# The last wait of a decode block: SyncE's queue or GpSimd's

## The chip, the cores and the metric

The kernel runs on one core of a Trainium2 chip. The metric is the device time of one execution in microseconds. Every comparison is of this time; the profile of one execution says where it goes. Engines carry the profile's names: PE is TensorE, DVE is VectorE, ACT is ScalarE, POOL is GpSimd and SP is SyncE. A q behind a name (SPq, POOLq) means the engine's own queue: waits, semaphores, branches and the issuing of DMAs.

## The reference

One step of decoding for 8 sequences: layer norm, attention over the last 1,024 cached positions (32 query heads, 4 key and value heads of 128), the output projection with a residual, then layer norm and a gated feed-forward block (GELU) with a second residual. All is float32.

```
W = min(4096, max(256, Sk // 4))
q = (x @ wq).reshape(B, Sq, Hq, Dh).transpose(0, 2, 1, 3)
k = repeat(k_cache[:, :, Sk - W:, :], rep, axis=1)
v = repeat(v_cache[:, :, Sk - W:, :], rep, axis=1)
p = softmax(einsum("bhqd,bhkd->bhqk", q, k) * (Dh ** -0.5))
attn = einsum("bhqk,bhkd->bhqd", p, v).transpose(...).reshape(B, Sq, Hq * Dh) @ wo
h = x + attn                                  # x was normalized ahead of wq
h2 = h + (gelu(n @ w_gate) * (n @ w_up)) @ w_down      # n = layernorm(h); Dm 1024, Df 3584
```

## The kernel before

The work is fourteen passes over 111 MB of weights and cache (`q0` to `d1` in `PASSES`), which SyncE's queue loads in turn into the two halves of one SBUF buffer, `w`. A pass's load waits until TensorE has used up the half that it goes into; TensorE multiplies the pass that has landed by a small stationary tile, `st`, into PSUM banks; VectorE, ScalarE and GpSimd turn the sums into the next stationary tile. Each engine has its own instruction stream, written out by hand, and semaphores alone order them: `pe`, `dve`, `act` and `pool` count what their engine has done, `s_in` and `s_dn` count what DMAs have landed.

The end is what the change touches. The last four of the down projection's 28 chunks arrive in small transfers (`s_dn`), and TensorE multiplies each as it lands. VectorE adds the last products to `pre` in two parts of `o_fin`, 160 and 96 columns. Then:

- ScalarE issues the store of the first part (L480) and, when the second is written (`s_fin`), adds 1 to `s_end` (L481).
- SyncE issues the store of the second part when `s_fin` says so (L482, L483).
- GpSimd, when `pre` is done, adds 1 to `s_end` (L485).
- SyncE waits for both counts in `s_end` (L486), clears the program's semaphores up to `s_fin` for the next execution (L487), and waits on L488 until both stores have landed: each adds 16 to `s_out`, and the wait takes the 32 away again.

L488 is the last line of `decode_block`. Lines at 569 are the opening that the framework puts ahead of a program.

Of the kernel before, what the change touches and what calls it, by code (L numbers as in the profile page):

```python
# [115 lines left out]
def decode_block(nc, out, x, srcs, W):  # L116
# [19 lines left out]
    s_out = nc.alloc_semaphore("s_out")  # L136
# [348 lines left out]
    nc.gpsimd.wait_ge(*t_pre).then_inc(s_end, 1)  # L485
    nc.sync.wait_ge(s_end, 2).then_inc(s_end, -2)  # L486
    nc.sync.sem_clear(range(first.num, s_fin.num + 1))  # L487
    nc.sync.wait_ge(s_out, 32).then_inc(s_out, -32)  # L488


# [93 lines left out]
```

## Time and profile before

| | us |
|---|---|
| time before, median of 3 runs | 263.91 |
| lowest and highest of the 3 | 263.84, 263.96 |
| time of the profiled execution | 263.77 |
| its span, from the program's first instruction to its last | 262.46 |
| what of its time lies outside the span | 1.31 |

The span is what all views speak of: they list the program's own instructions. The measured time is longer. The trace also records every change of a semaphore, and these records go on behind the span, where no view lists an instruction. One semaphore, number 2, is not the program's own. After TensorE's work is done it changes 18 times, in two passes of nine:

```
changes of semaphore 2 (ns from the span's start; steps since the change before)
pass 1: 260700  261247  261285  261329  262581  262624  262663  262697  262744
                  +547     +38     +44   +1252     +43     +39     +34     +47
pass 2: 263534  263569  263607  263650  263674  263779  263818  263852  263899
                   +35     +38     +43     +24    +105     +39     +34     +47
last changes of s_out: 262421 (the last of the stores' 32 counts), 262455 (taken away by L488)
```

Between the passes, from 262694 to 263310, nearly all semaphores of the core change once. A pass with the steps of pass 2, within 7 ns each, stands ahead of the program too and ends at 1 ns.

### The profile page before, as it was taken

How to read it: one execution, taken by the hardware profiler on the slowest of the kernel's cores; microseconds unless marked ns; L12 is line 12 of the kernel's file. 1: busy time of each engine (PE TensorE's matmuls, PEld its weight loads, DVE VectorE, ACT ScalarE, POOL GpSimd, SP SyncE). 2: the span in 40 equal slices, each digit the busy share in tenths (PEclk: the TensorE clock that was granted, in tenths of full speed). 3: DMA queues.
4: the chain of work that ended last, by engine and by line, in shares of the span. 5: the costliest groups of instructions: out<-in, count | busy, mean ns of one | idle time of the engine just before them, and what ended most of it. 6: DMA issues, size and time to landing. Idle time of an engine off the chain costs nothing. (4 is left out here: it accounts for less than half of the span.)

```text
span 262.5 us, 2187 instructions
## 1 busy us (share of the span) xinstructions
PE 136.8 (52%) x960; PEld 42.6 (16%) x960; DVE 35.9 (14%) x98; ACT 19.1 (7%) x28; POOL 6.8 (3%) x16
## 2 busy tenths in 40 slices
PE   0005905806826607627708608539277590585954
PEld 0001301201222102122102202112121130121321
DVE  0060110120130210110120100450101004003013
ACT  1030000000020000110000000210401010000000
POOL 2000100000000000000000100000000001001010
PEclk9999975955865965955956965957959598586899
DMA  8998997999899799989979989997999999799996
GB/s 320 484 410 390 479 479 340 459 479 410 390 479 479 340 459 479 420 380 479 479 330 469 479 380 420 479 479 320 479 434 405 439 479 479 320 454 424 439 390 230
DMA packets 3216, 111.31 MB, mean 424 GB/s; under 512 B 496, under 2 KB 784, under 8 KB 1040
## 3 DMA queue, kind: packets, MB, share of 16 engines
q1 hardware_dynamic: 3024, 111.20, 98.4%
q10 hardware_dynamic: 192, 0.11, 0.1%
HBM read 111.18 MB, written 0.13 MB: 424 GB/s over the span
## 5 line engine op out<-in xcount | busy, mean ns | idle before, releaser
L161 PE MATMUL banks<-w,st 128*32 128x512 f32 x864 | 125.3, 743 | 115.7 <-PEq L156 115.7
L161 PEld LDWEIGHTS banks<-w,st 128*32 128x32 f32 x864 | 34.3, 133 | 201.4 <-issue 201.4
L183 PE MATMUL banks<-ident,p 128*128 128x128 f32 x56 | 9.3, 321 | 6.3 <-PEq L156 6.3
L183 PEld LDWEIGHTS banks<-ident,p 128*128 128x128 f32 x56 | 7.4, 164 | 12.3 <-issue 12.3
L358 ACT ACTIVATE p<-banks,nmax 128x1024 f32<-128x1024 f32 x2 | 2.2, 1113 | 73.5 <-DVE nmax L98 73.5
L98 DVE TENSOR_REDUCE nmax<-banks 128x1 f32<-128x1024 f32 x2 | 2.5, 1225 | 33.8 <-PE banks L161 33.8
L98 DVE TENSOR_TENSOR y_sum<-y_sum,banks 128x512 f32<-128x512 f32 (+1 forms) x4 | 2.1, 552 | 33.6 <-PE banks L161 17.8
L98 DVE TENSOR_SCALAR q<-banks 128x512 f32<-128x512 f32 x2 | 1.4, 692 | 31.3 <-PE banks L161 31.3
L98 DVE TENSOR_TENSOR o_sum<-o_sum,banks 128x512 f32<-128x512 f32 x2 | 1.4, 690 | 29.5 <-ACT o_sum L371 29.5
L98 DVE TENSOR_TENSOR d_sum<-d_sum,banks 128x256 f32<-128x256 f32 (+1 forms) x3 | 1.4, 509 | 17.3 <-POOL d_sum L456 12.1
L397 POOL TENSOR_TENSOR y_sum<-y_sum,x_sb 128x256 f32<-128x256 f32 x1 | 0.7, 722 | 115.7 <-ACT y_sum L396 115.7
L422 POOL COPY st<-at 128x768 f32<-128x768 f32 (+2 forms) x3 | 1.8, 609 | 68.4 <-DVE at L98 68.4
L371 ACT COPY o_sum<-banks 128x512 f32<-128x512 f32 x2 | 1.2, 586 | 26.8 <-PE banks L161 26.8
L98 DVE TENSOR_TENSOR u0s<-u0s,banks 128x512 f32<-128x512 f32 x1 | 0.7, 689 | 16.3 <-ACT u0s L412 16.3
L98 DVE TENSOR_TENSOR g0s<-g0s,banks 128x512 f32<-128x512 f32 x1 | 0.7, 689 | 15.8 <-ACT g0s L412 15.8
L292 ACT ACT_TABLE_LOAD x2 | 2.6, 1283 | 1.7 <-POOL ident L264 1.6
L98 DVE TENSOR_TENSOR u1s<-u1s,banks 96x512 f32<-96x512 f32 x1 | 0.7, 683 | 14.0 <-ACT u1s L415 14.0
L221 PE MATMUL banks<-w,at 128*32 128x256 f32 x24 | 1.7, 387 | 1.5 <-DMA w<-weights 1.5
L313 ACT COPY st<-ln_t 128x1024 f32<-128x1024 f32 x2 | 2.1, 1046 | 5.1 <-DVE ln_t L98 5.1
L98 DVE TENSOR_TENSOR g1s<-g1s,banks 96x512 f32<-96x512 f32 x1 | 0.7, 682 | 10.9 <-ACT g1s L415 10.9
L98 DVE SCALAR_TENSOR_TENSOR o<-o_sum,share,o 128x128 f32<-128x128 f32 x6 | 2.1, 352 | 0.2
L412 ACT COPY u0s<-banks 128x512 f32<-128x512 f32 x1 | 0.6, 585 | 18.7 <-PE banks L161 18.7
(64 smaller groups left out, 39.5 us busy)
## 6 DMA issues: line engine op xcount, KB each, us to landing
w<-weights SPq DMA_DIRECT2D x2, 6144.0 KB, 23.5
w<-weights SPq DMA_DIRECT2D x2, 4096.0 KB, 24.5
w<-weights SPq DMA_DIRECT2D x1, 3072.0 KB, 17.0
w<-weights SPq DMA_DIRECT2D x2, 1024.0 KB, 20.1
w<-weights SPq DMA_DIRECT2D x1, 512.0 KB, 21.9
w<-weights SPq DMA_DIRECT2D x1, 320.0 KB, 22.3
w<-weights SPq DMA_DIRECT2D x1, 192.0 KB, 22.3
w<-weights SPq DMA_DIRECT2D x10, 28.9
```

Of the source, the lines that this page charges most:

```text
L98: ins = getattr(self.eng, n.name)(*n.args, **n.kw)
L161: ins = nc.tensor.matmul(bank(2 * s + c // 4)[32 * j:32 * j + 32, :], st[s][:, (c * NQ + j) * 32:(c * NQ + j + 1) * 32], w[:, at:at + N], ...
L183: ins = nc.tensor.transpose(pp[h][:, i], p_sb[:, c * P:(c + 1) * P], ident)
L221: ins = pe(lambda e: e.matmul(bank(7)[32 * j:32 * j + 32, 0:QW], at_[:, q, :], w[:, k:k + QW], start=(q == PAIRED), stop=(q == rows - 2)), ...
L292: t = act(lambda e: e.activation(sd, ve, AF.Sqrt), t_ve)
L313: act(lambda e: e.copy(to[1], wide), t, inc=False).then_inc(s_in[1], 2)
L358: t = act(lambda e: e.activation(p_sb, bank(0, 2), AF.Exp, bias=nmax, accum_out=tot), t)
L371: t = dve(lambda e: e.tensor_add(o_sum, o_sum, bank(3)), act(lambda e: e.copy(o_sum, bank(2)), done(f"v{hb}")))
L397: t = pool(lambda e: e.tensor_add(y_sum[:, 0:QW], y_sum[:, 0:QW], x_sb), t)
L412: t = act(lambda e: e.copy(out[:nb], bank(b)[:nb]), done(name))
L422: return nc.gpsimd.tensor_copy(st[s][:, at:at + n * 64].rearrange("p (c x m) -> p c x m", c=n, x=2), at_[:, c0:c0 + n].unsqueeze(2).to_bro ...
```

## The change

The wait on `s_out`, with the subtraction that goes with it, moves from SyncE's stream to GpSimd's. It stays the last line of the program. Nothing else changes: on every engine the instructions that compute, copy or issue a DMA are the same and stand in the same order. SyncE's last instruction is now the clearing on L487, and GpSimd's is this wait, right behind L485.

```diff
     nc.gpsimd.wait_ge(*t_pre).then_inc(s_end, 1)
     nc.sync.wait_ge(s_end, 2).then_inc(s_end, -2)
     nc.sync.sem_clear(range(first.num, s_fin.num + 1))
-    nc.sync.wait_ge(s_out, 32).then_inc(s_out, -32)
+    nc.gpsimd.wait_ge(s_out, 32).then_inc(s_out, -32)
```

## Rows read from the trace of the kernel before

**Rows 1.** The page: shares of the span by engine, and the weights' DMA queue.
```profile
PE 136.8 (52%) x960; PEld 42.6 (16%) x960; DVE 35.9 (14%) x98; ACT 19.1 (7%) x28; POOL 6.8 (3%) x16
...
q1 hardware_dynamic: 3024, 111.20, 98.4%
...
HBM read 111.18 MB, written 0.13 MB: 424 GB/s over the span
```

**Rows 2.** The chain that ended last, its end: start us, us, what.
```profile
237.35 22.27 DMA w<-weights
259.62 0.04 issue
259.66 0.52 PE banks L229 x8
...
260.28 0.54 DVE o_fin L98 x2
```

**Rows 3.** Busy time by engine in the last 1.5 us, its columns first.
```profile
core 0: us, PE busy (x) PEld busy (x) DVE busy (x) ACT busy (x) POOL busy (x), PEclk, DMA share, GB/s
...
261.00:262.50 1.50, 0.00 (x0) 0.00 (x0) 0.00 (x0) 0.00 (x0) 0.00 (x0) 0.74 0.32 87
```

**Rows 4.** The timeline, the two stores' issues: start us, us, queue and line.
```profile
260.63 0.35 ACTq L480 DMA_DIRECT2D out<-o_fin  x1
260.85 0.35 SPq L483 DMA_DIRECT2D out<-o_fin  x1
```

**Rows 5.** What writes `out`: duration ns min/median/max, first and last start.
```profile
L480 ACTq DMA_DIRECT2D out<-o_fin x1: 348/348/348, 260.6 to 260.6; - x1
L483 SPq DMA_DIRECT2D out<-o_fin x1: 348/348/348, 260.8 to 260.8; - x1
...
DMA to landing us min/median/max: 1.6/1.6/1.6
```

**Rows 6.** Line 488, the wait on the stores; columns as in rows 5.
```profile
L488 SPq EVENT_SEMAPHORE  x1: 17/17/17, 262.4 to 262.4; - x1
```

**Rows 7.** Waits of SyncE's queue, from 259: total us, times, longest.
```profile
SPq L483 <- DVE o_fin L98: 22.6, 1, 22.6
SPq L488 <- SPq L488: 1.1, 1, 1.1
```

**Rows 8.** Line 486, SyncE's wait on `s_end`.
```profile
L486 SPq EVENT_SEMAPHORE  x1: 17/17/17, 261.2 to 261.2; - x1
```

**Rows 9.** Line 487, SyncE's clearing of the semaphores.
```profile
L487 SPq EVENT_SEMAPHORE_RANGE_CLEAR  x1: 58/58/58, 261.3 to 261.3; - x1
```

**Rows 10.** GpSimd's timeline from 249 us to the end: its last work.
```profile
249.73 0.72 POOL L456 TENSOR_TENSOR d_sum<-d_sum,h_sb 128x256 f32<-128x256 f32 x1 [10.38 <-ACT d_sum L455]
256.85 0.39 POOL L390 COPY d_ex<-d_sum 64x256 f32<-64x256 f32 x1 [6.40 <-DVE d_sum L98]
```

**Rows 11.** Line 485, GpSimd's last instruction.
```profile
L485 POOLq EVENT_SEMAPHORE  x1: 17/17/17, 260.0 to 260.0; - x1
```

**Rows 12.** Line 276, two more waits on GpSimd's queue.
```profile
L276 POOLq EVENT_SEMAPHORE  x2: 17/17/17, 2.8 to 2.9; - x2
```

**Rows 13.** Line 481, ScalarE's last instruction.
```profile
L481 ACTq EVENT_SEMAPHORE  x1: 17/17/17, 261.0 to 261.0; - x1
```

**Rows 14.** Line 569, the opening: each engine's drain.
```profile
L569 SPq DRAIN  x1: 7/7/7, 0.0 to 0.0; - x1
L569 DVEq DRAIN  x1: 10/10/10, 0.1 to 0.1; - x1
L569 ACTq DRAIN  x1: 8/8/8, 0.1 to 0.1; - x1
...
L569 POOLq DRAIN  x1: 187/187/187, 0.3 to 0.3; - x1
```

## The prediction, made before the changed kernel ran

> **What bounds the kernel now.** I read the page's shares first. The queue that carries the weights takes 98.4% of the sixteen DMA engines' span, at 424 GB/s, while TensorE is busy 52% of the span and GpSimd 3% [rows 1]. The kernel is therefore bound by its weight stream. Nothing in the change touches that stream, so only the end can answer. I went there next with the chain that ended last: a landing of weights at 259.62 us, the last eight TensorE matmuls, and the two last VectorE sums, which end at 260.82 [rows 2]. The reader is to see that the chain as printed stops there: the remaining 1.64 us of the span hold no arithmetic on any engine. The stretch 261.00 to 262.50 has no busy instruction on any of the five and a DMA share of 0.32, which is the stores [rows 3].
>
> Then the stores. ScalarE issues one at 260.63 and SyncE the other at 260.85; each issue holds its queue for 348 ns and the median time to landing is 1.6 us [rows 4, 5]. The later one lands at 260.85 + 1.6 = 262.45, within rounding the end of the span (262.46). The instruction that sees it is the one that the change moves: the wait on L488, one record of 17 ns at 262.4 [rows 6], for which SyncE's queue stood 1.1 us [rows 7]. So the span ends when the second store has landed, and the wait costs the span 17 ns and nothing more.
>
> Last, what lies behind the span. The profiled execution took 263.77 us against a span of 262.46, so 1.31 us of the measured time lies outside it. No view lists instructions there. The updates of semaphore 2, shown with the time before, do: two passes of nine steps, the first waiting for SyncE (fourth step at 261.329, fifth at 262.581) and the second about a microsecond later. Both come after everything that the program does, and in them the change can cost something.
>
> **The change part by part.**
>
> *Taken from SyncE: one wait of 17 ns* [rows 6]. It is SyncE's last instruction and nothing is queued behind it. What SyncE does before it stays: the store, the wait on `s_end` (17 ns at 261.2) and the clearing of the semaphores (58 ns at 261.3) [rows 8, 9]. SyncE is then through at 261.3 + 0.06 = 261.4, about 1.1 us before the store lands, so its 17 ns leave the path.
>
> *Added to GpSimd: the same wait.* GpSimd's last arithmetic is the copy of 0.39 us at 256.85 [rows 10], and its last instruction is the wait on L485 at 260.0 [rows 11]. So GpSimd stands at the new wait from 260.0 on, long before the landing at 262.45, and is never late for it. Nothing is queued behind it, and nobody in the program waits for GpSimd after L485. A wait on GpSimd takes 17 ns in L485 [rows 11] and in two more on L276 [rows 12], the same as on SyncE. How soon it answers to its semaphore shows in the views to 0.1 us only. Term within the span: 17 − 17 = 0, with ±0.1 us as what the rows can resolve. I take 0, because the cover is complete: whoever looks, the store lands at the same moment.
>
> *Who closes the program.* This is the term that I do not take as nothing. In the first pass of semaphore 2 the five upward steps come at 260.700, 261.247, 261.285, 261.329 and 262.581. The last one follows SyncE's wait (updated at 262.455) by 126 ns; the second follows ScalarE's last instruction, its 17 ns wait on L481 at 261.0 [rows 13]; and four steps come back down 43, 39, 34 and 47 ns apart. So I read the pass as a line with SyncE at its far end, which the engines go up and down one after the other. TensorE starts it, ScalarE is second, and the two steps that follow 38 and 44 ns behind it are those of engines that were already there: VectorE, whose last sum ends at 260.82 [rows 2], and GpSimd, as third and fourth in some order. Before the change the last engine to come stands at the far end, and only the way back is left: 43 + 39 + 34 + 47 = 163 ns. After it the last to come is GpSimd. If GpSimd is third, a step up to the fourth, a step to SyncE and the whole way back remain. Their prices are in the second pass, where nobody is late: 43 + 24 + 105 + 39 + 34 + 47 = 292 ns. Difference: +129 ns. If it is fourth, 24 + 105 + 39 + 34 + 47 = 249 ns, +86 ns. The records don't name the engine of a step, so third is a choice: I take the dearer of two values that differ by 0.04 us. This term is +0.13 us, between +0.09 and +0.13.
>
> The Trainium skill ("Runtime: NRT & Kernel Launch", the section on the preamble and postamble breakdown) describes this as a serpentine over the five engines on the sync-barrier semaphore, about 355 ns, 44 ns a hop times eight. By that flat price two more hops up and down would be an estimate of 0.09 us instead of 0.13. The trace agrees with the sum (263.534 to 263.899 is 365 ns) but not with a flat hop: the turn at the far end took 105 ns where it followed at once, 43 ns where it was awaited.
>
> *GpSimd's own way out.* Between its wait and its step SyncE took 126 ns. GpSimd's is not shown, since it was long there when the line reached it. Below: it takes as long as SyncE, 0; I see no row by which it is quicker. Above: at the opening of the program, line 569, the same kind of instruction is drained in 7 ns on SyncE, 10 ns on VectorE and 187 ns on GpSimd, which had memsets in flight [rows 14]: a difference of 0.18 us if the way out holds such a drain and it costs the same. At the end GpSimd has nothing in flight (its last copy ended 5.2 us before the landing [rows 10]), so I stay near the lower end and take +0.03 us.
>
> *Sum.* Against the profiled execution: 263.77 + 0 (wait) + 0.13 (place in the line) + 0.03 (way out) = 263.93 us. The median of the three runs, 263.91, is 0.14 above the profiled one; the same 0.16 on it gives **264.07 us**, or +0.06%. With the ends of the terms the gain or loss is between 0.09 − 0.10 = −0.01 and 0.13 + 0.18 + 0.10 = +0.41 us, which is 263.90 to 264.32.
>
> **The rivals.** A measurement of this kernel tells a change from none beyond about 0.2%, here 0.53 us; "same" is what stays within it.
>
> *GpSimd's way out is long (slower).* Place: after GpSimd's wait, before its step. For it: GpSimd's drain at the opening was 27 times as long as SyncE's [rows 14], and the way out stood hidden before. Against it: all that is known is that GpSimd, done with its 17 ns at 260.0 [rows 11], had come when the line passed at 261.285 or 261.329, so its way out is at most about 1.3 us; and the two that are shown are short, SyncE's 126 ns and ScalarE's 0.21 us (from 261.0 + 0.02 [rows 13], 261.039 in the records' resolution, to 261.247). At the full 1.27 us instead of 0.126, the time would be 263.91 + 0.13 + 1.14 = 265.18. It decides the sign from 0.53 − 0.13 + 0.126 = 0.53 us of way out on. Chance 0.07.
>
> *SyncE alone ends the measured time (faster).* If what is timed ended with SyncE and did not wait for GpSimd, the end would move from 262.44 to the end of SyncE's clearing at 261.4 [rows 9], a gain of up to 1.06 us: 262.85. For it: 1.1 us is what SyncE stood [rows 7]. Against it: the steps of semaphore 2 show the engines leaving together, and the second pass begins only after the first has come down. Chance 0.03.
>
> *It makes no difference at all.* The passes could lie outside what is timed, or GpSimd's way out could be shorter than SyncE's 126 ns by just what the longer way back costs. Then the landing alone decides, as it did, and the time stays 263.91. For it: the store's 1.6 us [rows 5] are the same whoever waits. Against it: 1.31 us of the measured time lie outside the span, and the first pass is what lies next to it. Chance 0.12.
>
> **How the numbers follow.** The forecast, +0.09 to +0.41 us, has 0.78. Both it and the case of no difference are within 0.2%: 0.90. Slower by over 0.2% is the first rival, 0.07; faster is the second, 0.03. The three runs of before spread over 0.12 us. The range is 263.75 to 264.45: the case of no difference less that spread, 263.91 − 0.12 = 263.79, rounded outward, to the forecast's upper end plus it, 264.32 + 0.12 = 264.44. The two rivals that decide a sign lie outside it, 0.10 together, and I leave another 0.05 for what the views don't show.
>
> **What would show it.** In the changed profile the wait of 17 ns should stand on GpSimd's queue at about 262.4, SyncE's last record should be the clearing at about 261.3, and the span should be 262.5 ± 0.2. Issue, duration and landing of the two stores should be as before. The step of semaphore 2 that was late should be the third or fourth, with two quick ones above it, and the stretch from GpSimd's wait to the first pass's last step should be about 0.45 us (126 + 30 + 292 ns) instead of 0.29 (126 + 163 ns). The forecast is wrong if that stretch exceeds 0.8 us (a long way out), if the closing passes do not move with GpSimd (then SyncE alone counts), or if the stores land later, which would be a cause that I have not named.

## The result and the profile after

The changed kernel takes 264.62 us (median of 10 runs, 264.30 to 264.97) against 263.90 (10 runs): ratio 1.0027, 95% interval 1.0019 to 1.0035, slower by 0.72 us. The profiled execution took 264.58 us with a span of 262.70.

The page's shares and the weights' queue first, against [rows 1]: the weights flow as before. TensorE's busy time differs between the two executions (136.8 and 130.0 us); the weights' queue fills the span in both, and nothing here rests on it.

```profile
PE 130.0 (49%) x960; PEld 40.8 (16%) x960; DVE 35.9 (14%) x98; ACT 19.1 (7%) x28; POOL 6.8 (3%) x16
...
q1 hardware_dynamic: 3024, 111.20, 98.3%
...
HBM read 111.18 MB, written 0.13 MB: 424 GB/s over the span
```

The end of the chain that ended last (start us, us, what), against [rows 2]:

```profile
237.16 22.70 DMA w<-weights
259.86 0.04 issue
259.90 0.52 PE banks L229 x8
...
260.52 0.52 DVE o_fin L98 x2
```

Behind the last landing the same pieces follow, with durations within 0.02 us of those before; they end at 261.04, 0.22 us later. The two stores on the timeline, and what writes `out`, against [rows 4, 5]:

```profile
260.88 0.35 ACTq L480 DMA_DIRECT2D out<-o_fin  x1
261.07 0.35 SPq L483 DMA_DIRECT2D out<-o_fin  x1
```

```profile
L480 ACTq DMA_DIRECT2D out<-o_fin x1: 347/347/347, 260.9 to 260.9; - x1
L483 SPq DMA_DIRECT2D out<-o_fin x1: 347/347/347, 261.1 to 261.1; - x1
...
DMA to landing us min/median/max: 1.6/1.6/1.6
```

Issue (347 ns for 348) and landing are unchanged. The moved wait, line 488, against [rows 6], and SyncE's last instruction, line 487, against [rows 9]:

```profile
L488 POOLq EVENT_SEMAPHORE  x1: 17/17/17, 262.7 to 262.7; - x1
```

```profile
L487 SPq EVENT_SEMAPHORE_RANGE_CLEAR  x1: 58/58/58, 261.5 to 261.5; - x1
```

The wait is still 17 ns, seen when the second store lands (261.07 + 1.6). The reader is to see that the rows of the program's end are as they were, 0.25 us of span aside, and that these rows do not make 0.72 us: 264.58 − 262.70 = 1.88 us now lie outside the span, against 1.31 before. That is 0.56 us (1.876 − 1.315), and it is where no view looks. It is so in every run: in the 10 runs of the changed kernel the time less the span is 1.86 to 1.98 us. The records of semaphore 2 do:

```
pass 1, ns from the span's start      step 1  step 2  step 3  step 4  step 5  and back
before (SyncE waits)                  260700  261247  261285  261329  262581  262624  262663  262697  262744
after (GpSimd waits)                  260929  261487  263271  263315  263338  263428  263468  263502  263548
last instruction ends: before 262455 (SyncE), after 262704 (GpSimd)
```

The late step is the third, with two quick ones above it, so GpSimd is third in the line. But it comes 263271 − 262704 = 567 ns after GpSimd's wait, where SyncE's came 126 ns after its own.

The remaining 0.16 us of the 0.72 lie in the span (0.25 between the two profiled executions). The first matmuls on TensorE's timeline, before:

```profile
22.72 3.62 PE L161 MATMUL banks<-w,st 128*32 128x512 f32 x16 [22.72 <-PEq L156]
```

and after:

```profile
22.97 3.60 PE L161 MATMUL banks<-w,st 128*32 128x512 f32 x17 [22.97 <-PEq L156]
```

The difference of the two spans is complete when the first load has landed, 240 us ahead of the instruction that was changed. The repeats below take it up.

### The profile page after: what moved, and what is told of

Same layout as the page of the kernel before. It is cut to its first block, busy times and chain, and to the rows that moved or that the text cites. A ratio compares the mean times of both kernels' runs of the same rounds, so it can differ in the third digit from the quotient of the medians.

```text
span 262.7 us, 2187 instructions
## 1 busy us (share of the span) xinstructions
PE 130.0 (49%) x960; PEld 40.8 (16%) x960; DVE 35.9 (14%) x98; ACT 19.1 (7%) x28; POOL 6.8 (3%) x16
## 5 line engine op out<-in xcount | busy, mean ns | idle before, releaser
L161 PE MATMUL banks<-w,st 128*32 128x512 f32 x864 | 119.4, 713 | 122.7 <-PEq L156 122.7
L161 PEld LDWEIGHTS banks<-w,st 128*32 128x32 f32 x864 | 33.2, 128 | 203.4 <-issue 203.4
L183 PE MATMUL banks<-ident,p 128*128 128x128 f32 x56 | 8.5, 300 | 6.3 <-PEq L156 6.3
L183 PEld LDWEIGHTS banks<-ident,p 128*128 128x128 f32 x56 | 6.7, 152 | 12.3 <-issue 12.3
L396 ACT COPY y_sum<-banks 128x512 f32<-128x512 f32 x1 | 0.6, 586 | 19.3 <-PE banks L161 19.3
```

The costliest lines, as they stand in the source:

```text
L161: ins = nc.tensor.matmul(bank(2 * s + c // 4)[32 * j:32 * j + 32, :], st[s][:, (c * NQ + j) * 32:(c * NQ + j + 1) * 32], w[:, at:at + N], ...
L183: ins = nc.tensor.transpose(pp[h][:, i], p_sb[:, c * P:(c + 1) * P], ident)
L396: t = act(lambda e: e.copy(y_sum, bank(0)), done("o0"))
```

## The experiments

The edits are to the kernel before. Each replaces or surrounds the last wait. In the table behind them, "way out" is the time from the end of the waiting engine's last instruction to its step, "rest" from there to the last step of pass 1; each is read from one profiled execution.

**ScalarE, VectorE, TensorE wait.** Three runs, each with another engine's name:

```diff
-    nc.sync.wait_ge(s_out, 32).then_inc(s_out, -32)
+    nc.scalar.wait_ge(s_out, 32).then_inc(s_out, -32)      # or nc.vector, nc.tensor
```

> ScalarE waits for the stores. Theory A (the engines leave in a line, and each has its own way out between its last wait and its step): ScalarE is second, so its step is late, four quick steps up and the whole way back follow: 38+43+24+105+39+34+47 = 330 ns against 163 with SyncE, and its way out is the 208 ns seen before against 126. The stretch from the wait to the end of the first pass is about 0.54 us (0.29 with SyncE, 0.84 with GpSimd) and the time about 263.90 + 0.25 = 264.15. Rival B (anybody but SyncE is dear, because SyncE leaves the program early): as with GpSimd, about 264.6. The start of the span, by A, has nothing to do with it: span 262.5 and runs within 0.15 us of each other; if the scatter of the spans over 0.6 us is due to SyncE leaving early, it is here too.

> VectorE waits for the stores. Theory A: VectorE is fourth in the line, 24+105+39+34+47 = 249 ns from its step to the end of the first pass against 163; its way out has not been seen, I expect between SyncE's 126 and ScalarE's 208: stretch 0.38 to 0.46 us, time 264.0 to 264.1. Rival B (anybody but SyncE is dear): about 264.6. Scatter of spans: small by A, about 0.6 us if SyncE leaving early causes it.

> TensorE waits for the stores. Theory A (place in the line, and a way out of each engine's own): TensorE is first, so the whole line of 365 ns is left behind its step, against 163 with SyncE; its way out has not been seen, I expect 0.13 to 0.17 us as on the three others that are short. Stretch from the wait's end to the end of the first pass 0.50 to 0.54 us, against 0.29, so the measured time lies 1.53 to 1.57 us above the span (1.32 with SyncE) and the median is about 264.17. Rival D (the way out is long on every engine that stands at the far side of the line from SyncE): 264.5 or more.

Line 488 of each, ScalarE:

```profile
L488 ACTq EVENT_SEMAPHORE  x1: 17/17/17, 262.6 to 262.6; - x1
```

VectorE:

```profile
L488 DVEq EVENT_SEMAPHORE  x1: 21/21/21, 262.5 to 262.5; - x1
```

TensorE:

```profile
L488 PEldq EVENT_SEMAPHORE  x1: 51/51/51, 262.6 to 262.6; - x1
```

ScalarE: 264.10 us against 263.95, ratio 1.0008 (0.9999 to 1.0017). VectorE: 264.04, 1.0005 (0.9996 to 1.0014). TensorE: 264.30 against 263.99, 1.0012 (1.0003 to 1.0021). All three steps were late where the line puts them: second, fourth, first. The records of the three, whose span ends where the wait ends:

```
ns from the span's start   wait ends   own step   end of pass 1   profiled time, us
ScalarE                    262567      262701     263019          264.05
VectorE                    262515      262684     262933          263.96
TensorE                    262647      262883     263236          264.31
```

From the records and each profiled execution:

```
who waits   place   way out   rest   both    time less span   time less span less both
SyncE       5       126 ns    163    289     1.315 us         1.03 us
VectorE     4       169       249    418     1.445            1.03
ScalarE     2       134       318    452     1.483            1.03
TensorE     1       236       353    589     1.663            1.07
GpSimd      3       567       277    844     1.876            1.03
```

The last column is the point. What lies outside the span is the waiting engine's way out, its rest of the line, and 1.03 us that do not depend on who waits (0.04 more for TensorE). Theory A stands in all five; that any engine but SyncE is as dear as GpSimd does not. ScalarE's way out was expected at 208 ns and took 134, and TensorE's was expected at 130 to 170 and took 236: the line was right, the ways out have to be measured one by one. The two time intervals of ScalarE and VectorE include no change; what sets them apart from SyncE is the records. The calm that theory A expected did not come either: ScalarE's runs spread over 0.62 us, but so did those of the kernel before beside them, over 0.59 (28 runs).

**One more wait on GpSimd.** SyncE waits for the stores; does a longer stream of GpSimd alone cost something?

```diff
+    nc.gpsimd.wait_ge(*t_pre)
     nc.gpsimd.wait_ge(*t_pre).then_inc(s_end, 1)
```

> The kernel before, with one more wait on GpSimd, on the same condition and ahead of the one it has; SyncE waits for the stores as before. GpSimd's stream is as long as in the changed kernel. Theory A: no change, 263.90, span 262.5, runs within 0.15 us. Rival C (the longer stream of GpSimd, another place of its code, is what makes the span longer and scattered by 0.6 us): median of the span about 262.7, time about 264.1, scattered.

263.88 us, ratio 1.0001 (0.9992 to 1.0010). The run does not test what it was made for: the two waits became one instruction, as line 486 shows (43 ns instead of 17), so the stream had no more instructions than before. Its runs spread over 0.59 us, not the expected 0.15.

```profile
L486 POOLq EVENT_SEMAPHORE  x1: 43/43/43, 260.1 to 260.1; - x1
```

The mended form raises a semaphore of its own (`s_two`) with the first wait and takes it down with the second (the line that allocates `s_two` is not shown, here and below):

```diff
+    nc.gpsimd.wait_ge(*t_pre).then_inc(s_two, 1)
+    nc.gpsimd.wait_ge(s_two, 1).then_inc(s_two, -1)
     nc.gpsimd.wait_ge(*t_pre).then_inc(s_end, 1)
```

> The kernel before, with two more waits on GpSimd that are satisfied when they are reached, ahead of the one by which it tells SyncE that it is done, this time of a kind that cannot become one instruction. SyncE waits for the stores. GpSimd's stream is longer than in the changed kernel. Theory A: time as before, 263.97, spans in the mean as before, 262.65. Rival C (a longer stream of GpSimd lengthens or scatters the span): spans 0.1 us or more longer in the mean. GpSimd's step must still be hidden: it ends some 0.2 us later than before and has 0.7 us of room.

263.93 us against 263.95, ratio 0.9999 (0.9990 to 1.0008); spans 262.59 us in the mean, those of before beside it 262.59. Two more instructions in GpSimd's stream are not the cause.

**Both wait.** GpSimd waits for the stores and hands on to SyncE, which is then late too:

```diff
+    nc.gpsimd.wait_ge(s_out, 32).then_inc(s_two, 1)
+    nc.sync.wait_ge(s_two, 1).then_inc(s_two, -1)
     nc.sync.wait_ge(s_out, 32).then_inc(s_out, -32)
```

> GpSimd waits for the stores, then hands on to SyncE, which also waits: both leave late, SyncE some 0.05 to 0.1 us after GpSimd. Theory A: GpSimd's way out of 567 ns still sets the end and hides SyncE's, so the stretch from GpSimd's wait to the end of the first pass is 0.84 us as in the changed kernel, and so are 0.55 us of the 0.72; if SyncE's early leaving makes the other 0.17 and the scatter, these are gone and the time is about 264.45 with runs within 0.15 us; if not, 264.6 and scattered. Rival B (it is SyncE's absence that is dear): about 264.0, by the hand-over of 0.1 us alone.

264.58 us, ratio 1.0029 (1.0017 to 1.0041). GpSimd's wait, line 489, and SyncE's last, line 491:

```profile
L489 POOLq EVENT_SEMAPHORE  x1: 17/17/17, 262.6 to 262.6; - x1
```

```profile
L491 SPq EVENT_SEMAPHORE  x1: 17/17/17, 262.8 to 262.8; - x1
```

GpSimd's step came at 263221, 567 ns behind the end of its wait (262654), and SyncE's, 24 ns after the fourth, cost nothing extra. So it is GpSimd's presence at the end that is dear, not SyncE's absence. The spans were not calmer (262.7 to 263.4), so SyncE's early leaving does not explain their scatter.

**Twice, and three times.** Is it 567 ns from GpSimd's last instruction, or from its waking?

```diff
-    nc.sync.wait_ge(s_out, 32).then_inc(s_out, -32)
+    nc.gpsimd.wait_ge(s_out, 32)
+    nc.gpsimd.wait_ge(s_out, 32).then_inc(s_out, -32)
```

> GpSimd waits for the stores twice, one wait behind the other on the same condition; the second takes the counts away. Theory A (567 ns are what GpSimd needs from its last instruction to its step, whatever that instruction is): 567 ns from the end of the second wait, which stands about 0.1 us behind the first as the two waits on line 276 do; the time lies 1.87 us above the span, the span itself is 0.1 us longer, and the time is about 0.1 us above the changed kernel's. Rival E (567 ns run from the moment GpSimd wakes, and an instruction more fits in them): about 0.47 us from the second wait, and the time as in the changed kernel.

264.50 us, ratio 1.0023 (1.0014 to 1.0032). Again the two became one instruction of 43 ns, and the way out was 567 ns from its end; the question stayed open. The form that cannot be joined:

```diff
-    nc.sync.wait_ge(s_out, 32).then_inc(s_out, -32)
+    nc.gpsimd.wait_ge(s_out, 32).then_inc(s_two, 1)
+    nc.gpsimd.wait_ge(s_two, 1).then_inc(s_two, -1)
+    nc.gpsimd.wait_ge(s_out, 32).then_inc(s_out, -32)
```

> GpSimd waits for the stores, then for a semaphore that this first wait raised, then once more for the stores: three waits that cannot become one instruction. Theory A (567 ns from the last instruction of GpSimd, whatever it is): 567 ns from the end of the third wait, which ends about 0.2 us behind the first (two waits on line 276 stood 0.1 us apart); time about 0.2 us above the changed kernel's, 264.75. Rival E (567 ns run from the moment GpSimd wakes, and instructions more fit in them): about 0.37 us from the third wait, time as in the changed kernel, 264.55.

264.69 us against 263.95, ratio 1.0027 (1.0017 to 1.0038). Its first wait ended at 262569, its third, line 491, at 262761, and GpSimd's step came at 263328: 567 ns behind the third again. The instructions ahead are paid on top; nothing of the way out runs under them. GpSimd stood less than 0.1 us for this third wait (the second ended at 262665), so the 567 ns are not the price of the last wait's having been long either.

**GpSimd leaves later, hidden.** SyncE waits for the stores; GpSimd's own signal waits for `s_fin`:

```diff
-    nc.gpsimd.wait_ge(*t_pre).then_inc(s_end, 1)
+    nc.gpsimd.wait_ge(s_fin, 1).then_inc(s_end, 1)
```

> The kernel before, but GpSimd adds to the count that SyncE waits for when the second part of the result is written, not when the sums ahead of it are: it leaves about 0.85 us later, having stood less long, and SyncE still waits for the stores. Theory A (567 ns always): GpSimd's step, the third, comes about 0.58 us behind its wait, later than ScalarE's by more than the quick 38 ns, and it is hidden behind SyncE's: time as before, 263.95. Rival F (567 ns are the price of waking after a long stand, or of the stores' own semaphore): the third step follows ScalarE's by 38 ns; time as before as well.

Line 485 stands 1 us later than in [rows 11], and SyncE's wait on the stores is as in [rows 7]:

```profile
L485 POOLq EVENT_SEMAPHORE  x1: 17/17/17, 261.0 to 261.0; - x1
```

```profile
SPq L488 <- SPq L488: 1.1, 1, 1.1
```

263.94 us against 263.99, ratio 0.9997 (0.9988 to 1.0006). The third step came at 261622, 572 ns after the wait's end (261050) and 177 ns after ScalarE's instead of 38. The long way out is there with another semaphore; it only costs nothing while SyncE is later still. The run does not test the long stand: GpSimd's copy ended at 257420, so it stood 3.6 us for this wait, longer than the 2.5 us for the stores in the changed kernel (260235 to 262687). The three waits above do.

**GpSimd works behind its wait.** The changed kernel, with a fill of a scratch tile as GpSimd's last instruction, 128 x 1024 or 128 x 1:

```diff
-    nc.sync.wait_ge(s_out, 32).then_inc(s_out, -32)
+    nc.gpsimd.wait_ge(s_out, 32).then_inc(s_out, -32)
+    nc.gpsimd.memset(sb("scratch", [P, 1024]), 0.0)        # or [P, 1]
```

> The changed kernel, and behind its last wait GpSimd fills a scratch tile of 128 x 1024 that nobody reads (an operation added to the computation; one like it took 0.95 us). It asks what the 567 ns hold. Theory A1 (the way out ends a drain of GpSimd's cores, and counts from the end of their work): third step about 0.5 us behind the end of the fill, time about 1 us above the changed kernel's, 265.5. Rival A2 (the 567 ns are the queue's alone, and do not look at the cores): third step about 0.6 us behind the wait, in the middle of the fill, and the time as in the changed kernel, 264.6, with a span 1 us longer.

> As the run with the long fill, with a scratch tile of 128 x 1, whose fill takes about 0.1 us (an operation added). Theory A1 (the way out counts from the end of the cores' work): step 0.5 to 0.57 us behind the fill, some 0.15 to 0.3 us later than in the changed kernel, time 264.7 to 264.85. Rival A2 (the queue's alone): later by the issue of one instruction at most, under 0.1 us, time 264.6.

The end of GpSimd's timeline with the long fill:

```profile
262.68 0.95 POOL L489 MEMSET scratch<- 128x1024 f32 x1 [5.33 <-POOLq L488]
```

and with the short one:

```profile
262.64 0.10 POOL L489 MEMSET scratch<- 128x1 f32 x1 [3.85 <-POOLq L488]
```

Long: 265.53 us against 263.95, ratio 1.0058 (1.0043 to 1.0073), step 3 at 264145, 513 ns after the fill's end. Short: 264.66, ratio 1.0026 (1.0017 to 1.0036), step 3 at 263249, 512 ns after the fill's end. In both, the way out counts from the end of the fill and takes 0.51 us from there. From the end of the wait the steps come 1570 and 716 ns later, so a way out of 567 ns that looks at the queue alone (A2) is excluded; the short fill's time lies just under the 264.7 to 264.85 that A1 expected. What is left of the time less the span, without way out and rest, is 1.08 and 1.04 us.

**The changed kernel again**, on the same chip as three of the runs above (TensorE waits, the two joined waits, GpSimd leaves later).

> The changed kernel again, beside the kernel before on the same chip. Theory A: the time lies 1.87 us above the span (1.32 before) in every run; the spans are the same for both kernels in the mean, 262.4 to 263.0 each, and the 0.17 us of the first comparison that lay in the span were chance: ratio about 1.0021, 0.55 us. Rival G (the change also lengthens the span): ratio 1.0027 again, with the spans' median 0.15 us above those of before.

264.56 us against 263.99, ratio 1.0023 (1.0013 to 1.0033): 0.57 us. The time less the span is 1.88 us in its profile, as in the first; over all runs it is 1.86 to 1.99 us (mean 1.92 of 9) against 1.29 to 1.43 (mean 1.35 of 32), with spans on record to 0.1 us. This difference of 0.57 us is the whole of the repeat's. Its spans are 262.71 us in the mean of 9 runs (262.5 to 263.1), those of before beside it 262.67 in 32 runs (262.4 to 263.4). The 0.04 us are well inside their scatter. And four profiled spans, less the time of their first matmul, agree to 0.02 us: 262.46 − 22.72 (before), 262.58 − 22.83 (this run), 262.65 − 22.92 (GpSimd leaves later), 262.70 − 22.97 (after) are 239.73 to 239.75. The profiles of five more runs whose span ends with one wait instruction on SyncE, GpSimd, ScalarE or VectorE give the same 239.73 to 239.75; the first matmul of the nine starts at 22.72 to 23.04, in each 0.135 us behind the last count of the first load's semaphore. So the profiled spans differ by when the first load lands, and the last wait has no part in it. That the wider scatter of the runs without a profile has the same source is likely, but not shown.

## Why the prediction was wrong

*The bound and the span: right.* The weights set the span, the moved wait costs it 17 ns as before, and the stores land 1.6 us after their issue.

*The place in the line: right.* It was put at +0.13 us with GpSimd third. GpSimd is third, and the term measured 277 − 163 = 114 ns. That it is third was luck in part: the records of before left third or fourth open, and the dearer was taken. The flat price of the Trainium skill ("Runtime: NRT & Kernel Launch", the section on the preamble and postamble breakdown), 44 ns a hop, stated there for the barrier ahead of a program, gave an estimate of 0.09 us. The measured 114 ns lie between that estimate and the 0.13.

*GpSimd's own way out: this step failed.* It was put at +0.03 us and bounded at +0.18. It measured 567 − 126 = +0.44 us. Of the 0.55 us between the forecast of 264.07 and the measured 264.62 this term makes 0.41; most of the rest is the 0.16 us of span. The bound came from the opening's drains, 187 ns against 7 [rows 14], taken as if the way out could hold no more than such a drain. No row said that. The bound that did stand in the records was written down beside it, in the rival: up to 1.3 us, since the line reached GpSimd that long after its last wait. The sum should have kept that end, and the range with it. (The chance of 0.78 was put on +0.09 to +0.41 us, though the sum's own lower end was −0.01; neither holds the measured +0.72.) With the measured sizes the sum is 0 + 0.11 + 0.44 = 0.55 us, which is what the time less the span shows (1.876 − 1.315 = 0.56) and the repeat (0.57).

*The rivals.* The first, a long way out, was the right mechanism with its place and its price from 0.53 us on; it was given 0.07. Its sign came too: the stretch from GpSimd's wait to the end of the first pass is 567 + 277 = 844 ns, over the 0.8 us named in the prediction. That SyncE alone ends the time is excluded: with GpSimd late the whole closing moved. That the closing makes no difference is excluded by the table's last column.

*The runs' spread.* Three runs within 0.12 us were taken as the kernel's scatter. The kernel before spans 263.75 to 264.34 in 28 runs and 263.69 to 264.70 in 32, the spans moving with it. The 0.16 us that the first comparison shows beyond 0.56 fit that scatter and were not there in the repeat; that they were chance is the likely reading, not a shown one.

*Still open.* What GpSimd does in the half microsecond behind its last work is not in any record here, nor why it is 567 ns behind a wait and 512 behind a fill.

## What to carry to other kernels

In every run here the last instruction of the program is followed by a closing that the profile's views don't list: compare the measured time less the span, and look at who arrives last. Give the last wait to the engine that leaves fastest and stands at the far end of the closing line, here SyncE; none of the four others was faster, and GpSimd costs 0.56 us, though it looked free. When a cost was hidden before, take its upper bound from the time in which it was hidden, not from a row of something that resembles it.

## What the runs showed of the hardware

GpSimd needs 567 ns from its last wait to its step in the closing in five runs of four kernels (572 in a fifth kernel), and 512 to 513 ns from the end of a fill; SyncE 126, ScalarE 134, VectorE 169, TensorE 236. ScalarE's step before the change came 208 ns after its last instruction, without having stood for it, against 134 after standing 1.4 us, so an engine's way out is not one fixed number. In nine profiled executions the first matmul starts at 22.72 to 23.04 us and what follows to the end of the span takes 239.73 to 239.75 us: the start, not the end, makes these spans differ.
